# Attention with relative bias and a mixture of adapters: the last pair's values by key group, the last batch's mixture written out apart, and two batches' mixture moved sooner

## The chip, the cores and the metric

The kernel runs on one core of one Trainium2 chip. The time is device microseconds of that core for one execution. It is the median of several runs; lower is better.

## The reference

Two layers follow one another. First comes attention over 8 batches, 8 heads, 576 positions and 64 dimensions a head, with a bias that depends on the distance of two positions:

```python
scores = scale * np.matmul(q, k.transpose(0, 1, 3, 2))
...
scores = scores + bias.transpose(2, 0, 1)[None, :, :, :]
scores = scores - np.max(scores, axis=-1, keepdims=True)
attn = np.exp(scores)
attn = attn / (np.sum(attn, axis=-1, keepdims=True) + 1e-09)
return np.matmul(attn, v).astype(np.float32)
```

Its output, 4608 rows of 512 columns (8 heads of 64), goes row by row through a mixture of 8 adapters of rank 16, of which the two with the largest logits count:

```python
logits = x @ w_gate
topk = np.argpartition(-logits, K, axis=1)[:, :K]
...
        z = x[mask] @ A[e]
        delta[mask] += w[mask, k, None] * (z @ B[e])
return (x + delta).astype(np.float32)
```

Here w is the softmax over a row's two chosen logits, and K is 2.

## The kernel before

**Tiling.** The work goes by pairs: a pair is one batch and two heads (e = 0 and 1, heads hp and hp + 4), so there are 32 pairs, four to a batch. The 576 positions are 512 and a tail of 64. A pair's scores come in five key groups: groups 0 to 3 are 128 keys each against 512 queries of both heads; group 4 takes the tail's keys and queries together. For each group `qk` makes the scores on TensorE, `expo` (L351) takes the exponential on ScalarE, and `band` (L357) multiplies the biased diagonal band on VectorE. `pv` (L372) multiplies the probabilities by the values, one slot of 128 queries (sl) after the other, over all five key groups; a column of ones beside the values gives the sums. `recip` and `norm` (L408, L416) divide and write x, the attention's output in bf16. It has two accumulators for a pair: part 0 for slots 0 to 2 and part 1 for slot 3 and the tail.

**The mixture of a batch b** follows once its four pairs are done. x must be transposed: by a transposing DMA for batches 1 to 5 (`m_xdma`, L441), by 16 TensorE transposes and two VectorE copies for batches 0, 6 and 7 (`m_x`, L447). The tails of two batches are handled together, with the odd batch (`m_xtail`, L458, in float32 by plain matmuls). Then come `m_logits` (L469: 16 or 20 matmuls, the two largest logits on VectorE), `m_gate` (L490: an exponential on ScalarE, a product on GpSimd, a sum and reciprocal on VectorE, the normalised gate on GpSimd), `m_z` (L510: x times A, weighed by the gate on VectorE), `m_zT` (transposes of z), `m_out` (L537: z times B on TensorE, x added on VectorE, and a transfer of half the rows after every second of four) and `m_outt` (L549) for the tails.

**Order.** It is written by hand. One loop (L605) runs over slots n = 5 i + g, for pair i and group g. A slot issues qk of slot n + 1, the exponential of slot n, then band work of slot n - 1, then the previous pair's `pv`, at g = 1, 2 and 3. The mixture's steps are put into slots by a table of events (`mixture`, L569): at (di, g) after the pair 4 (b + 1). The number d, 3 for batches up to 5 and 2 after that, says how many pairs later the logits stand. What falls behind the last slot runs in order after the loop, which goes five slots past the last exponential.

Each engine takes its instructions in this order and waits where one isn't ready. Score tiles have two buffers in PSUM (L66). All other matmul outputs share four ("acc", L67): transposes, values, logits, z and outputs each take the next of these in turn, and wait until VectorE has read what stood there. Instructions on VectorE go through a recorder, so the profile gives all of them line 87; they are told apart by their tiles: kqT, p (the band), rc, x, xT, m, zt, zT, o, ot.

Of the kernel before, what the change touches and what calls it, by code (L numbers as in the profile page):

```python
# [10 lines left out]
FP32 = mybir.dt.float32  # L11
BF16 = mybir.dt.bfloat16
AX = mybir.AxisListType
ALU = mybir.AluOpType
# [13 lines left out]
def kernel(  # L28
# [14 lines left out]
    nc = tc.nc  # L43
    B, H, S, D = q.shape
    NB = bias_table.shape[0]
    Dm = H * D
    E = moe_w_gate.shape[1]
    r = moe_A.shape[2]
    ER = E * r
    HP = H // 2  # L50
    D1 = D + 1
    scale = 1.0 / float(np.sqrt(D))
    S4 = 512
# [37 lines left out]
    dve = Recorder(nc.vector)  # L91
# [280 lines left out]
    def pv(i, sl):  # L372
# [25 lines left out]
        for g in range(4):  # L398
# [4 lines left out]
        mm(acc[:, c:c + 2, :], p4[:, sl * 128:(sl + 1) * 128],  # L403
           vt[:, hp, :].rearrange("p (e d) -> p e d", e=2), False, True)

    rcs = {}

    def recip(i, part):  # L408
        if i % HP == 0 and part == 0:
            xs[i // HP] = xp.tile([128, 9, HP, D], BF16, name="x", tag="x", bufs=4)  # L410
        n = 6 - 3 * part
        rc = sp.tile([128, n], FP32, name="rc", tag=f"rc{part}")
        dve.reciprocal(rc, pvs[(i, part)][:, :, D])
        rcs[(i, part)] = rc

    def norm(i, part):  # L416
        b, hp = divmod(i, HP)
        n = 6 - 3 * part
        dve.tensor_tensor(xs[b][:, 6 * part:6 * part + n, hp, :],
                          pvs.pop((i, part))[:, :, :D],  # L420
                          rcs.pop((i, part)).unsqueeze(2)
                          .to_broadcast((128, n, D)), op=ALU.mult)

    def x_rows(b):
        return xs[b][:, 0:8].rearrange("p (t e) c d -> p t (e c d)", e=2)

    def x_tail(b):
        return xs[b][:, 8].rearrange("p c d -> p (c d)")
# [9 lines left out]
    def new_xT(b):  # L438
        st[(b, "xT")] = xp.tile([128, 20, 128], BF16, name="xT", tag="xT")
# [16 lines left out]
        dve.tensor_copy(st[(b, "xT")][:, half * 8:half * 8 + 8, :], ps)  # L456

    def m_xtail(b):  # L458
        ps = acp.tile([128, 4, 128], FP32, name="xtps", tag="acc")
        for c in range(4):  # L460
            e, hh = divmod(c, 2)
            for bb in range(2):
                nc.tensor.matmul(ps[:, c, bb * 64:(bb + 1) * 64],
                                 lhsT=x_tail(b - 1 + bb)[:, hh * 128:(hh + 1) * 128],
                                 rhs=ident[:, e * 64:(e + 1) * 64],
                                 start=(c + bb == 0), stop=True, skip_group_check=True)
        dve.tensor_copy(st[(b, "xT")][:, 16:20], ps)

    def m_logits(b):  # L469
        nt, xT = tiles(b), st[(b, "xT")]  # L470
        lp = acp.tile([128, nt, E], FP32, name="lp", tag="acc")
        first = True
        for t in range(nt):
            for c in range(4):
                nc.tensor.matmul(lp[:, t, :], lhsT=xT[:, 4 * t + c, :],
                                 rhs=Wb[:, c, :], start=first, stop=(c == 3),
                                 skip_group_check=True)
                first = False
        m8 = sp.tile([128, nt, 8], FP32, name="m8", tag=f"m8{nt}")
        for t in range(nt):  # L480
            dve.max(out=m8[:, t, :], in_=lp[:, t, :])
        df = sp.tile([128, nt, E], FP32, name="df", tag=f"df{nt}")
        dve.tensor_tensor(df, lp, m8[:, :, 0:1].to_broadcast((128, nt, E)),
                          op=ALU.subtract)
        mk = sp.tile([128, nt, E], FP32, name="mk", tag=f"mk{nt}")
        dve.tensor_tensor(mk, lp, m8[:, :, 1:2].to_broadcast((128, nt, E)),
                          op=ALU.is_ge)
        st[(b, "g")] = dict(df=df, mk=mk)

    def m_gate(b, part):  # L490
        nt, d = tiles(b), st[(b, "g")]
        if part == 0:
            ex = sp.tile([128, nt, E], FP32, name="ex", tag=f"ex{nt}")
            nc.scalar.activation(ex, d["df"], ACT.Exp)
            d["ex"] = ex
        elif part == 1:
            nc.gpsimd.tensor_tensor(d["mk"], d["mk"], d["ex"], op=ALU.mult)
        elif part == 2:
            sm = sp.tile([128, nt], FP32, name="sm", tag=f"sm{nt}")
            dve.tensor_reduce(sm, d["mk"], axis=AX.X, op=ALU.add)  # L500
            dve.reciprocal(sm, sm)
            d["sm"] = sm
        else:
            gate = sp.tile([128, nt, E], BF16, name="gate", tag=f"gate{nt}")
            nc.gpsimd.tensor_tensor(
                gate, d["mk"], d["sm"].unsqueeze(2).to_broadcast((128, nt, E)),
                op=ALU.mult)
            d["gate"] = gate
# [55 lines left out]
            nc.sync.dma_start(out=out[n0:n0 + 64, :], in_=o[e * 64:(e + 1) * 64])  # L564


    events = {}

    def mixture(b):  # L569
        tail = b % 2 == 1  # L570
        i0 = HP * (b + 1)

        def at_slot(di, g, f, *a):
            events.setdefault(5 * (i0 + di) + g, []).append((f, a))

        if 0 < b < B - 2:
            at_slot(0, 4, m_xdma, b)
        else:
            at_slot(0, 4, m_x, b, 0)
            at_slot(0, 4, m_x, b, 1)  # L580
        if tail:
            at_slot(1, 4, m_xtail, b)
        d = 3 if b < B - 2 else 2
        at_slot(d, 0, m_logits, b)
        for n in range(4):
            at_slot(d, (2, 3, 4, 4)[n], m_gate, b, n)
        at_slot(d + 1, 0, m_z, b, 0, 4)
        if tail:
            at_slot(d + 1, 2, m_z, b, 4, 5)
        at_slot(d + 1, 4, m_zT, b)  # L590
        at_slot(d + 2, 0, m_out, b, 0)
        at_slot(d + 2, 2, m_out, b, 1)
        at_slot(d + 3, 0, m_out, b, 2)
        at_slot(d + 3, 2, m_out, b, 3)
        if tail:
            at_slot(d + 4, 4, m_outt, b)
# [5 lines left out]
        mixture(b)  # L602
    transposes(0)
    qk(0)
    for n in range(NG + 5):  # L605
        i, g = divmod(n, 5)
        b, hp = divmod(i, HP)
        nb = b + 1
        if n + 1 < NG:
            qk(n + 1)  # L610
        if n < NG:
            expo(n)

        if i >= HP and nb < B and hp in (1, 2) and g in (0, 2):
            behind_dve(load_v(nb, (2 * hp - 2 + g // 2,))[0])
        if b + 2 < B and (hp, g) in ((2, 4), (3, 1)):
            if g == 4:
                alloc_kq(b + 2)
            behind_dve(load_kq(b + 2, ws=(int(g == 1),))[0])
        if hp == 3 and g < 4 and nb + 1 < B:  # L620
            load_tail(nb + 1, g // 2, g % 2)
        if hp == 1 and g in (1, 3) and nb < B:
            load_tail(nb, 2, g // 2)
        if 22 <= n < 27:
            load_weights(n - 22)
        if n in (11, 13, 15, 18):
            cast_v((11, 13, 15, 18).index(n), dve)
        if n in (8, 10, 12, 15):
            band_table((8, 10, 12, 15).index(n))
        if 9 <= n < 15:  # L630
            band(2 * n - 18)
            band(2 * n - 17)
        if 16 <= n <= NG:
            band(n - 1)
        if n == 10 or g == 1 and hp == 0 and 0 < i < NPAIR:
            tail_scores(b)
        if n in (12, 13):
            load_tail(1, n - 12, 0)
            load_tail(1, n - 12, 1)
        if n == 6:  # L640
            tail_transposes(0)
        if n in (0, 3):
            cast_kq(1 + n // 3, 0, dve)
            cast_kq(1 + n // 3, 1, dve)
        if g == 0 and 3 <= i + 2 < NPAIR:
            behind_dve(cast_kq(i + 2, 0))
        if (n in (0, 4, 12) or g == 0 and i > 2) and i + 1 < NPAIR:
            transposes({0: 1, 4: 2, 12: 3}.get(n, i + 1))
        if n == 18 or g == 2 and hp == 2 and 0 < b < B - 1:
            tail_transposes(nb)  # L650
        if 13 <= n < 19:
            for sl in ((3, 4), (0, 1, 2))[n % 2]:
                pv((n - 13) // 2, sl)
            recip((n - 13) // 2, 1 - n % 2)
            norm((n - 13) // 2, 1 - n % 2)
        if i > 3:
            if g == 1:
                pv(i - 1, 0)
                pv(i - 1, 1)
            if g == 2:  # L660
                pv(i - 1, 2)
                recip(i - 1, 0)
            if g == 3:
                pv(i - 1, 3)
                pv(i - 1, 4)
                recip(i - 1, 1)
        if g == 2 and 3 <= i + 2 < NPAIR:
            behind_dve(cast_kq(i + 2, 1))
        if g == 2 and HP <= i < NPAIR:
            behind_dve(cast_v(i))  # L670
        if i > 3 and g in (2, 4):
            norm(i - 1, g // 2 - 1)
        for f, a in events.pop(n, ()):
            f(*a)
# [33 lines left out]
```

The softmax here doesn't subtract the row's maximum and nothing guards it: scores larger than these inputs give would overflow.

## Time and profile before

| | before |
|---|---|
| time, median of 3 runs | 210.39 us (209.14 to 211.6) |
| span of the profiled run | 209.4 us, mean TensorE clock 0.952 |
| TensorE matmul busy | 178.6 us (85%) |
| VectorE busy | 172.5 us (82%) |
| ScalarE busy | 160.7 us (77%), of it 152.9 in 160 exponentials |
| GpSimd busy | 103.3 us (49%) |
| DMA | 40.65 MB, 194 GB/s on average |

The span runs from the first to the last instruction. Busy is the time in which an engine executes; for TensorE it can flatter, since matmuls overlap. A share is over the whole span, whose stages have different limits: a start of some 40 us in which the loads come in, a loop, and an end after the last exponential. A line of a timeline or of the chain gives start and length in us, the engine, the source line, the operation, and then output and input by the program's names. A bracket at its end gives how long the engine stood idle before it and which instruction released it.

### The profile page before, as it was taken

The page shows a single profiled execution, that of the slowest core. Times are in us where ns is not written, and L with a number is a line of the kernel's source. Part 1 is how long each engine was busy: PE and PEld are TensorE (multiplying, and loading weights), DVE is VectorE, ACT ScalarE, POOL GpSimd, SP SyncE. Part 2 cuts the span into 40 slices and gives each one's busy share as a digit, 9 for nine tenths or more (in the row PEclk, how much of TensorE's full clock was granted, in tenths as well). Part 3 has the DMA queues.
Part 4 walks back from the last instruction along what each step waited for, and adds up shares of the span by engine and source line. Part 5 has one row for each costly group of instructions (what it writes and reads, how often), then busy time and mean ns, then how long its engine had stood idle before and what let it go on. Part 6 is the DMA issues. An engine that isn't in the chain of part 4 may idle for free.

```text
span 209.4 us, 6933 instructions
## 1 busy us (share of the span) xinstructions
PE 178.6 (85%) x2768; PEld 120.5 (58%) x2768; DVE 172.5 (82%) x450; ACT 160.7 (77%) x187; POOL 103.3 (49%) x187
## 2 busy tenths in 40 slices
PE   1784399898889999999999999999997999998560
PEld 0241287666666666666666666667665676666420
DVE  3524699999878997999889998999798679988862
ACT  4698356989989898999799889987997688991000
POOL 7693494796745375447554664466543341120000
PEclk9999679999999999999999999999999699999955
DMA  5989999799889699999999999999999640222406
GB/s 186 220 167 160 297 293 157 202 276 151 103 274 235 115 216 261 292 179 214 264 310 164 176 220 304 196 175 203 281 263 167 189 139 3 103 103 53 200 0 250
DMA packets 84504, 40.65 MB, mean 194 GB/s; under 512 B 64240, under 2 KB 81808, under 8 KB 84472
## 3 DMA queue, kind: packets, MB, share of 16 engines
q1 hardware_dynamic: 66080, 38.02, 73.8%
q0 software_dynamic: 18112, 2.17, 19.9%
q8 instruction: 21, 0.34, 0.7%
q14 instruction: 11, 0.09, 0.2%
q10 hardware_dynamic: 280, 0.02, 0.1%
HBM read 29.97 MB, written 9.45 MB: 188 GB/s over the span
## 4 chain that ended last, share of the span: by engine, by line
PE 37%; DVE 22%; DMA 18%; ACT 12%; issue 4%; POOL 3%; SPq 2%; DVEq 0%; POOLq 0%; ACTq 0%
ACT p L354 10%; PE pv L382 9%; PE sc L333 9%; DVE p L87 6%; DMA xT<-x 6%; DVE o L87 4%; DMA kf<-in_k_dram 4%; PE kqps L293 4%; PE sc L339 4%; DMA Wb<-in_moe_w_gate_dram 4%; PE zp L519 3%; DVE x L87 3%; DMA vf<-in_v_dram 3%; DVE kqT L87 2%; DMA g_d<-gg 2%
## 5 line engine op out<-in xcount | busy, mean ns | idle before, releaser
L354 ACT ACTIVATE p<-sc 128x1024 bf16<-128x1024 f32 x160 | 152.9, 1028 | 18.9 <-PE sc L339 9.6
L87 DVE TENSOR_TENSOR p<-p,M 128x512 bf16<-128x512 bf16 (+1 forms) x128 | 66.3, 540 | 0.1
L382 PE MATMUL pv<-vn,p 128*128 128x65 bf16 (+1 forms) x1280 | 60.0, 197 | 0.0
L382 PEld LDWEIGHTS <-p 128*128 128x128 bf16 (+1 forms) x1408 | 51.2, 101 | 14.4 <-issue 9.5
L333 PE MATMUL sc<-kqT 64*128 64x512 bf16 x256 | 51.7, 403 | 7.9 <-ACT p L354 7.1
L146 POOL CAST kqn<-qf 128x512 bf16<-128x512 f32 x29 | 18.1, 624 | 43.6 <-DVE rc L87 41.8
L87 DVE TENSOR_TENSOR x<-pv,rc 128x384 bf16<-128x384 f32 x64 | 29.0, 453 | 1.2
L146 POOL CAST kqn<-kf 128x512 bf16<-128x512 f32 x29 | 18.4, 634 | 23.5 <-DVE xT L87 6.3
L293 PE MATMUL kqps<-ident,kqn 128*128 128x128 bf16 x256 | 21.9, 231 | 8.2 <-DVE kqn L87 4.7
L87 DVE COPY kqT<-kqps 128x1024 bf16<-128x1024 bf16 x32 | 21.9, 684 | 8.4 <-PE kqps L293 8.1
L382 PE MATMUL pv<-vt,p 128*128 128x130 bf16 x128 | 28.5, 222 | 0.0
L333 PEld LDWEIGHTS <-kqT 64*128 64x128 bf16 x256 | 12.7, 94 | 24.8 <-issue 17.9
L293 PEld LDWEIGHTS <-kqn 128*128 128x128 bf16 x256 | 15.5, 102 | 16.7 <-DVE kqn L87 5.9
L150 POOL CAST vn<-vf 128x512 bf16<-128x512 f32 x28 | 21.2, 758 | 6.2 <-DVE rc L87 6.2
L87 DVE TENSOR_TENSOR o<-dl,x 128x512 f32<-128x512 f32 x32 | 21.5, 681 | 1.2 <-PE dl L540 1.2
L87 DVE RECIPROCAL rc<-pv 128x6 f32<-128x6 f32 x64 | 11.6, 181 | 7.0 <-PE pv L382 6.8
L339 PEld LDWEIGHTS <-kqT 128*128 128x128 bf16 x128 | 10.1, 99 | 7.6 <-issue 2.7
L540 PE MATMUL dl<-Bb,zT 128*128 128x512 bf16 x32 | 12.4, 411 | 1.5 <-DVE zT L87 1.5
L339 PE MATMUL sc<-kqT,tlT 128*128 128x512 bf16 x32 | 12.4, 389 | 1.1 <-ACT p L354 1.0
L339 PE MATMUL sc<-tlT,kqT 128*128 128x128 bf16 x128 | 12.6, 222 | 0.0
L339 PE MATMUL sc<-B,ident 128*128 128x128 bf16 x64 | 9.1, 222 | 1.8 <-POOL B L258 1.8
L136 POOL DMA_DIRECT2D vt<-in_v_dram x16 | 10.1, 636 | 0.0
(78 smaller groups left out, 180.2 us busy)
## 6 DMA issues: line engine op xcount, KB each, us to landing
vf<-in_v_dram SPq DMA_DIRECT2D x128, 64.0 KB, 4.0
out_dram<-o SPq DMA_DIRECT2D x16, 512.0 KB, 3.0
kf<-in_k_dram SPq DMA_DIRECT2D x6, 1024.0 KB, 7.1
qf<-in_q_dram SPq DMA_DIRECT2D x6, 1024.0 KB, 10.1
kf<-in_k_dram SPq DMA_DIRECT2D x8, 256.0 KB, 4.5
qf<-in_q_dram SPq DMA_DIRECT2D x8, 256.0 KB, 4.8
out_dram<-ot SPq DMA_DIRECT2D x8, 128.0 KB, 5.0
Mr<-g_d SPq DMA_DIRECT2D x4, 192.0 KB, 4.5
```

Source lines behind the costliest of these rows:

```text
L87: self.last = f(*a, **kw)
L136: nc.gpsimd.dma_start(out=o, in_=sr[e])
L146: return (eng or nc.gpsimd).tensor_copy(o, s)
L150: return (eng or nc.gpsimd).tensor_copy(vns[b % 2][:, :, hp:H:HP, :D], vfs[b][:, :, hp:H:HP, :])
L293: nc.tensor.transpose(o, n[:, w, j], ident)
L333: nc.tensor.matmul(sc[:, h * 512:(h + 1) * 512], lhsT=t[s, 0, g * 128:(g + 1) * 128], rhs=t[s, 1, :], start=True, stop=True)
L339: nc.tensor.matmul(o, lhsT=lhsT, rhs=rhs, start=start, stop=stop, skip_group_check=True)
L354: nc.scalar.activation(p, scs.pop(n), ACT.Exp, scale=scale)
L382: nc.tensor.matmul(o, lhsT=lhsT, rhs=rhs, start=start, stop=stop, skip_group_check=True)
L519: nc.tensor.matmul(zp[:, t - t0, :], lhsT=xT[:, 4 * t + c, :], rhs=Ab[:, c, :], start=(t == t0 and c == 0), stop=(c == 3), skip_group_chec ...
L540: nc.tensor.matmul(ps, lhsT=zT[:, t, :], rhs=Bb, start=True, stop=True)
```

## The change

There are three parts.

1. The last pair (31): its values are multiplied by key group as the probabilities come (`pv_group`), two groups in each of the last two slots of the loop and only group 4 behind the last exponential. Both parts are then normalised in a row.
2. The last batch (7) has its mixture written out apart (`m_last`). The column blocks that come from its first two pairs (even blocks) are transposed already at pair 31, the others (odd blocks) at the end (`m_xh`), with the copy shared between VectorE and ScalarE. z is multiplied before the gate is known. The first two tiles are weighed with the gate not yet divided by its sum, which is made good when x is added; the other tiles take the divided gate, and their x is added by TensorE and the result copied by ScalarE. Each quarter of the rows leaves by a transfer of its own, from the scores' buffers.
3. Batches 5 and 6: batch 5 is transposed on TensorE instead of by DMA, and for both the logits stand at (1, 3) instead of (3, 0) and (2, 0), with the later steps following sooner. Their outputs end within the loop. All tails (odd batches) are now transposed in bf16 by 4 TensorE transposes instead of 8 float32 matmuls.

The loop now ends one slot past the last exponential. The diff, cut:

```diff
+    def pv_group(i, g):
...
+        for sl in range(4):
+            acc, c = pvs[(i, sl // 3)], 2 * (sl % 3)
+            if g == 4:
+                mm(acc[:, c:c + 2, :], p4[:, sl * 128:(sl + 1) * 128],
+                   vt[:, hp, :].rearrange("p (e d) -> p e d", e=2), False)
+                continue
+            for e in range(2):
+                o = e * 512 + sl * 128
+                mm(acc[:, c + e, :], probs[(i, g)][:, o:o + 128],
+                   vn[:, g, e * HP + hp, :], sl % 3 == 0 and g == 0 and e == 0)
...
     def m_xtail(b):
-        ps = acp.tile([128, 4, 128], FP32, name="xtps", tag="acc")
...
+        ps = acp.tile([128, 2, 2, 128], BF16, name="xtps", tag="acc")
+        for hh in range(2):
             for bb in range(2):
...
+                nc.tensor.transpose(ps[:, hh, bb, :],
+                                    x_tail(b - 1 + bb)[:, hh * 128:(hh + 1) * 128], ident)
...
+    def m_xh(b, odd):
...
+        for t in range(4):
+            for h in range(2):
+                c = 2 * h + odd
+                nc.tensor.transpose(ps[:, t, h, :], x[:, t, c * 128:(c + 1) * 128], ident)
...
+        if odd:
+            dve.tensor_copy(o[:, 0:2], ps[:, 0:2])
+            nc.scalar.copy(o[:, 2:4], ps[:, 2:4])
+        else:
+            dve.tensor_copy(o, ps)
...
+    def m_last(b):
+        m_xh(b, 1)
+        m_xtail(b)
+        m_logits(b)
...
+        zps = [acp.tile([128, n, ER], FP32, name="zp", tag="acc") for n in (4, 1)]
...
+        m_gate(b, 0)
+        wt = d["mk"]
+        dve.tensor_tensor(wt, wt, d["ex"], op=ALU.mult)
...
+        weigh(0, 2, zps[0][:, 0:2], wt[:, 0:2])
...
+        dve.tensor_reduce(sm, wt, axis=AX.X, op=ALU.add)
+        dve.reciprocal(sm, sm)
...
+        weigh(2, 4, zps[0][:, 2:4], wn[:, 0:2])
+        weigh(4, 5, zps[1], wn[:, 2:3])
...
+        for t0, t1 in ((0, 2), (2, 5)):
+            ps = acp.tile([128, t1 - t0, 128], BF16, name="ztps", tag="acc")
+            for t in range(t0, t1):
+                nc.tensor.transpose(ps[:, t - t0, :], zt[:, t, :], ident)
+            (nc.scalar.copy if t0 else dve.tensor_copy)(zT[:, t0:t1], ps)
+            dl = scp.tile([128, 2, Dm], FP32, name="sc", tag="sc")
+            for t in range(t0, t0 + 2):
+                nc.tensor.matmul(dl[:, t - t0], lhsT=zT[:, t, :], rhs=Bb, start=True,
+                                 stop=(t0 == 0))
+                if t0:
+                    nc.tensor.matmul(dl[:, t - t0], lhsT=ident, rhs=x[:, t], start=False,
+                                     stop=True)
+            for t in range(t0, t0 + 2):
+                if t0:
+                    nc.scalar.copy(o[:, t], dl[:, t - t0])
+                else:
+                    dve.scalar_tensor_tensor(o[:, t], dl[:, t], sm[:, t:t + 1], x[:, t],
+                                             op0=ALU.mult, op1=ALU.add)
+                nc.sync.dma_start(out=orr[:, t], in_=o[:, t])
+        st[(b, "zT")] = zT
+        m_outt(b)
...
-        if 0 < b < B - 2:
+        if b == B - 1:
+            at_slot(-1, 0, m_xh, b, 0)
+            at_slot(0, 1, m_last, b)
+            return
+        if 0 < b < B - 3:
             at_slot(0, 4, m_xdma, b)
...
+        if b >= B - 3:
+            if tail:
+                at_slot(1, 1, m_xtail, b)
+            at_slot(1, 3, m_logits, b)
+            for n in range(4):
+                at_slot(*((1, 4), (2, 0), (2, 0), (2, 0))[n], m_gate, b, n)
+            at_slot(2, 1, m_z, b, 0, 4)
+            if tail:
+                at_slot(2, 2, m_z, b, 4, 5)
+            at_slot(2, 4, m_zT, b)
+            for t in range(4):
+                at_slot(3, (0, 1, 3, 4)[t], m_out, b, t)
+            if tail:
+                at_slot(4, 1, m_outt, b)
+            return
...
-    for n in range(NG + 5):
+    for n in range(NG + 1):
...
+        if n >= NG - 2:
+            for pg in ((0, 1), (2, 3), (4,))[n - NG + 2]:
+                pv_group(NPAIR - 1, pg)
+        if n == NG:
+            for part in range(2):
+                recip(i - 1, part)
+                norm(i - 1, part)
```

## The prediction

> **What bounds the kernel now.** I read the page's picture in 40 slices first, to divide the run into a loop and an end.
>
> ```profile
> PE   1784399898889999999999999999997999998560
> ...
> DVE  3524699999878997999889998999798679988862
> ACT  4698356989989898999799889987997688991000
> ...
> PEclk9999679999999999999999999999999699999955
> ```
>
> A slice is 5.2 us. From about 40 us on, TensorE, VectorE and ScalarE are all nine tenths busy; ScalarE then has nothing for the last 20 us. Two things stand out: a dip of the TensorE clock in slice 32, far inside the loop, and the half clock of the last two slices. So I asked for busy times by stage (columns: length, then busy time and count of PE, weight loads, DVE, ACT, POOL, then clock, DMA share, GB/s).
>
> ```profile
> 122.20:143.60 21.40, 20.82 (x339) 14.22 (x337) 19.49 (x53) 19.68 (x23) 11.54 (x21) 1.00 1.24 224
> ...
> 161.00:167.40 6.40, 5.13 (x79) 3.53 (x80) 3.93 (x15) 4.01 (x6) 2.06 (x3) 0.73 0.68 173
> 167.40:189.50 22.10, 21.46 (x353) 15.11 (x352) 20.01 (x57) 20.04 (x22) 5.93 (x13) 1.00 0.23 83
> 189.50:209.40 19.90, 10.01 (x136) 6.24 (x132) 12.36 (x32) 0.24 (x2) 0.52 (x2) 0.76 0.37 133
> ```
>
> The first row is one ordinary batch (four pairs): TensorE 20.82 of 21.40 us, VectorE 19.49, ScalarE 19.68. TensorE sets the pace, with the other two some 10% behind: 0.6 us a batch is all the room TensorE has. The last row is the end: 19.9 us in which no engine is full, so a chain sets it. The 161 to 167.4 row is the clock dip. The chain of waits says what is in it (start, length, what), and ScalarE's timeline what it cost.
>
> ```profile
> 150.27 11.72 DMA xT<-x
> 161.98 0.05 issue
> 162.03 0.68 PE lp L475 x20
> ```
>
> ```profile
> 158.94 2.85 ACT L354 ACTIVATE p<-sc 128x1024 bf16<-128x1024 f32 x3 [0.62 <-PE sc L339]
> 163.29 1.02 ACT L354 ACTIVATE p<-sc 128x1024 bf16<-128x1024 f32 x1 [1.49 <-PE sc L333]
> ...
> 165.10 1.02 ACT L354 ACTIVATE p<-sc 128x1024 bf16<-128x1024 f32 x1 [0.67 <-PE sc L333]
> 166.36 2.86 ACT L354 ACTIVATE p<-sc 128x1024 bf16<-128x1024 f32 x3 [0.23 <-PE sc L339]
> ...
> 182.69 6.81 ACT L354 ACTIVATE p<-sc 128x1024 bf16<-128x1024 f32 x7 [0.16 <-ACT ex L494]
> ```
>
> Batch 5's transposing DMA lands 11.7 us after its issue begins, behind the moment at which its logits stand first in TensorE's queue. TensorE waits 1.07 us, its clock falls (0.73 on average until 167.4), and ScalarE loses 1.49 + 0.67 + 0.23 = 2.4 us. In batches 1 to 4 the logits start at 75.1, 96.5, 118.0 and 139.3 with no such wait. The last exponential ends at 182.69 + 6.81 = 189.5 us; call this T. From there the chain of waits goes on:
>
> ```profile
> 192.38 0.56 DVE x L87
> ...
> 195.21 1.20 DVE o L87 x2
> 196.41 0.61 DVE xT L87
> 197.02 0.05 issue
> 197.06 0.27 PE lp L475 x4
> ...
> 204.11 0.68 DVE o L87
> 204.79 0.60 DVEq L703
> ```
>
> Between T and the last logits (T + 7.8) stand not only the last pair's values and transposes but batch 6's outputs ("o", 0.68 us each). The tail's copy ends at 205.4 (T + 15.9), and 4.0 us of output transfer follow.
>
> **What the Trainium skill says.** "TensorE: Matmul & The Clock Gate", section "HAM oscillation", warns of TensorE gaps over about 3.4 us; here a wait of 1.07 us was enough to be followed by the slow clock, so the trace is stricter. The same page, section "Part 4: PE-mode transpose", gives about 275 ns for a transpose inside a kernel; the trace has 16 of them in 0.89 us (56 ns each, pipelined), which I use. "ScalarE: Activation LUTs", section "What ACT_TABLE_LOAD costs", gives 186 ns + 0.833 ns per element: 612 ns for 512, and the trace has 597 for the 128x512 activation from PSUM; I use it for the new ScalarE copies (an estimate of 506 ns for 384). "VectorE: DVE Perf Modes", section "The perf-mode tier table", caps a float PSUM source lower than a bf16 one: the trace agrees, 678 against 414 ns for 512 elements.
>
> **The change, part by part.**
>
> *Batch 5 without the DMA.* Takes away the wait and the slow clock: -2.4 us at T. Its two transposes add 16 matmuls, 0.89 us, and two VectorE copies, 2 x 0.68 = 1.36 us.
>
> *Batch 5's and 6's mixture sooner.* Inside the loop moving costs nothing in the sum; what counts is what crosses T. Batch 6's transposes of z (0.32 us on TensorE, 0.41 on VectorE), four output matmuls (0.22 to 0.32 each, 1.0 together) and three of its four output additions (2.04 on VectorE) come to stand before T, and batch 5's tail copy (0.68, at 189.75 in the trace) with them.
>
> *Last batch's even column blocks at pair 31.* 8 transposes, 0.45 us, and one copy, 0.68, before T instead of after.
>
> *Last pair's values by key group.* Before, its 46 matmuls stand behind T although four fifths of their inputs are ready. 32 of them (9 take 0.30 us, so 1.1) go before T. The rest, some 0.5 us, stay behind the last exponential.
>
> *Tail transposes in bf16.* 4 instead of 8 matmuls, -0.1 us before T; its copy 0.41 instead of 0.68.
>
> Sum for TensorE before T: 0.89 + 0.32 + 1.0 + 0.45 + 1.1 - 0.1 = 3.6 us. With the engine 97% full I give no credit for its idle time (0.6 us a batch, two batches: at best 1.2). T moves by -2.4 + 3.6 = +1.2, to 190.7. Check for VectorE: 39.7 us busy from 143.6 to 189.5, plus 1.36 + 0.41 + 2.04 + 0.68 + 0.68 - 0.27 = 4.9, gives 44.6 in 47.1 us, 95%: possible, but nearly a second bound. If it holds TensorE up through the four accumulators, T is 192; with all TensorE room used it is 189.8.
>
> *Added waits.* All of batch 5's and 6's gate runs in one slot: VectorE's sum now waits for GpSimd's product, with the bias products queued behind it; but GpSimd's cast ahead (0.61) and product (0.26) are shorter than VectorE's own copy and its wait, so about nothing. In the last slot batch 6's fourth output matmul waits for an accumulator that VectorE's normalisation of pair 30 frees; key group 4 and so everything later is behind it. I put that matmul at T, and its addition on VectorE (0.68) ahead of the last reciprocal.
>
> *From T to the last logits.* The fourth addition ends at T + 1.0; reciprocal and normalisations (0.19 + 0.56 + 0.17 + 0.35, the trace's own) to T + 2.3; transposes to T + 2.65; half the odd copy on VectorE (0.41) and the tail's (0.41), the other half on ScalarE (0.6) beside them, to T + 3.2; the last logits (0.27) T + 3.5. Before: T + 7.8. Gain 4.3.
>
> *From the logits to the tail's copy.* Before 8.1 us (197.3 to 205.4). After, in a row: maxima 0.5, difference 0.2, exponential with its handover 0.35, product now on VectorE 0.25, first z weighing 0.4, sum, reciprocal and gate 0.65, two weighings 0.6, first copy of z 0.3: 3.3. TensorE then does two output matmuls and only behind them the other three transposes: at the half clock (0.43 a matmul, as 201.67 to 203.56 shows) 1.35; ScalarE copies z, 0.55; then four matmuls, the tail's one and its four (1.7 + 1.1), and the tail's copy 0.7. About 8.6: a loss of 0.5, since the outputs' additions, now shared with ScalarE, no longer bound it but TensorE's row does. At full clock it would be 7.3.
>
> *The transfer.* Before, 1.3 MB goes out in the last 5 us; after, the pieces leave as they come and the last 256 KB meet an emptier queue. Bounded by 4.0 (as now) and 3.0 (the landing time of the larger outputs inside the loop, on the page's list of transfers); I take 3.2: -0.8.
>
> Sum: +1.2 - 4.3 + 0.5 - 0.8 = -3.4 us; 210.39 - 3.4 = 207.0.
>
> **Rivals.**
>
> *More room than I grant.* TensorE's idle shares absorb 1.2 us of the added work and the end runs at full clock: -3.4 - 1.2 - 1.3 gives 204.5. For it: ScalarE runs unbroken in the last seven slots, so TensorE keeps up there. Against: its busy share is 97% in every stage.
>
> *VectorE takes the place of TensorE.* T at 192.4 instead of 190.7, and its queue runs late into the end, 0.7 more: 209.4, no change. For it: 95% by my own sum, and a stretch (172.4 to 177.4) in which it is already 5.00 of 5.00 us busy just where batch 6's transposes sit, as batch 5's now will. Against: most of its work has a slot or more of slack.
>
> *A new stall in the loop (slower).* Pair 24 gets 0.89 us more on top of z, tail scores and transposes, pair 26 gets batch 5's z with the next tail transposes: if a wait on an accumulator idles TensorE for a microsecond and the clock falls as it did at 162, twice, that is 2 x 2.4 lost, and the end may gain only 3.2: +1.2 + 4.8 - 3.2 = +2.8, 213.2. Against: pair 28 of the kernel before has the same load with no clock dip.
>
> **How the numbers follow.** My forecast 0.55, more room 0.22, VectorE 0.14, new stall 0.09. Range: the loop from +0.3 to +2.5, the end from -6.0 to -3.2, and 0.7 for the spread of the times before (209.14 to 211.6); taken together not all at their worst, 204.2 to 209.4. Faster by over 1% means under 208.3: most of my forecast and all of the second, 0.77; within 1% the rest of it and VectorE's case, 0.14; slower 0.09.
>
> **What would show it.** The TensorE clock at 1.0 through 160 to 168, no wait for a transposing DMA by batch 5's logits; last exponential at about 190.7 (189.8 to 192); no output addition of batch 6 after T + 1.0; last logits at T + 3.5; the second group of output matmuls at half clock; last copy at T + 12.1. I am wrong if ScalarE shows new idle time of over a microsecond in pairs 24 to 27, if VectorE's queue reaches T more than a microsecond late, or if other runs of the kernel before have no stall in batch 5, so that nothing is removed.

## The result, and the profile after

The changed kernel takes 217.58 us (median, 214.95 to 217.97) against 210.07 for the kernel before: ratio 1.032, with a 95% interval of 1.022 to 1.043. Measured a second time, beside the experiments (e5), the ratio was 1.028 (1.019 to 1.036). All ratios leave out the executions that are over 1.5% above the fastest of their kernel, on both sides, so a ratio can differ from the quotient of two medians. The forecast was 207.0, faster. It is slower.

The picture in 40 slices of the changed kernel (a slice is 5.4 us), with the rows of TensorE, ScalarE and the clock:

```profile
PE   1586398898999999999999899989989899886860
...
ACT  3499356899989898989798889876877898783110
...
PEclk9998579999999999999999999979999999999558
```

The half clock of the end is still there (slices 38 and 39), the dip inside the loop has moved from slice 32 to slice 27, and after it no engine keeps its row of nines: from slice 27 to 36 TensorE shows 8 or 9 and ScalarE mostly 6 to 8.

To compare kernels I cut each trace at three marks that every kernel has: ScalarE's tail exponential of pair 24, that of pair 28, and the end T of the last exponential. A is pairs 24 to 27, B is pair 28 to T, C is T to the end. First A and B of the kernel before (its C is the last row of stages in the prediction), then A of the kernel of experiment e4, which has no late DMA, then the changed kernel (busy times by stage; columns as in the prediction):

```profile
146.41:170.18 23.77, 21.90 (x347) 14.91 (x344) 19.44 (x54) 19.66 (x23) 9.55 (x16) 0.93 0.98 222
170.18:189.50 19.32, 18.72 (x319) 13.03 (x315) 17.61 (x51) 18.22 (x20) 4.66 (x9) 1.00 0.17 68
```

```profile
145.68:166.93 21.25, 20.45 (x347) 14.15 (x344) 19.33 (x54) 19.52 (x23) 9.55 (x16) 1.00 0.98 221
```

```profile
150.38:175.01 24.63, 22.86 (x370) 15.88 (x369) 22.44 (x61) 20.20 (x22) 9.18 (x16) 1.00 0.72 208
175.01:196.13 21.12, 18.80 (x331) 13.49 (x329) 17.65 (x49) 18.13 (x20) 5.65 (x10) 1.00 0.17 56
196.13:215.70 19.57, 10.25 (x108) 6.27 (x106) 8.79 (x29) 2.38 (x5) 0.00 (x0) 0.70 0.30 104
```

A of the kernel before holds the stall; without one it is 21.25 us (e4). So A is 3.4 us longer, B 1.8 longer, and C, where the forecast had 4.6 to gain, 0.3 shorter. In A and B TensorE is idle for 1.8 and 2.3 us, with its clock at 1.00, against 0.8 in A of e4 and 0.6 in B of the kernel before. (In e5's trace of the same kernel, which has a few more matmul records, the idle times are 1.4 and 2.1.) In A there is also more work, 22.9 us busy against 20.45. B's busy time on TensorE has hardly grown (18.72 to 18.80, 19.02 in e5): what grew there is waiting.

The forecast -2.4 us for the stall did not come either. The chain of waits of the changed kernel, 20 us earlier than in the one before:

```profile
130.29 11.48 DMA xT<-x
141.77 0.05 issue
141.81 0.56 PE lp L525 x16
```

Batch 4's transposing DMA is late now (and batch 3's by a little), before anything of the change runs but the tail transposes of batches 1 and 3. So the changed kernel's trace holds a stall of the same kind as the one before; A, B and C, 4.9 us in sum over the undisturbed ones (those without a late DMA), are what is the change's own. The two traces are 6.3 us apart (209.4 and 215.7): these 4.9, 3.2 for late DMAs and 0.8 for a later start of the loop in the changed kernel's, less 2.5 for the late DMA in the one before. The traced execution of the kernel before lies 1.1 us above its median, which gives the 7.5 us between the medians.

### The profile page after: what moved, and what is told of

The parts are those of the page before. It is cut to its first block, busy times and chain, and to the rows that moved or that the text cites. A ratio compares the mean times of both kernels' runs of the same rounds, so it can differ in the third digit from the quotient of the medians.

```text
span 215.7 us, 6931 instructions
## 1 busy us (share of the span) xinstructions
PE 181.2 (84%) x2755; PEld 123.3 (57%) x2770; DVE 170.9 (79%) x453; ACT 163.5 (76%) x191; POOL 103.3 (48%) x185
## 4 chain that ended last, share of the span: by engine, by line
PE 42%; DMA 22%; ACT 14%; DVE 8%; issue 7%; POOL 3%; SPq 2%; POOLq 0%; another core or an unknown queue 0%; ACTq 0%; DVEq 0%
ACT p L354 12%; DMA xT<-x 11%; PE pv L382 10%; PE sc L333 10%; PE sc L339 5%; PE kqps L293 4%; PE zp L569 3%; DMA vf<-in_v_dram 3%; DMA qf<-in_q_dram 3%; DMA tl<-in_q_dram 3%; DMA kf<-in_k_dram 2%; DVE o L87 2%; DVE p L87 1%; DVE x L87 1%; PE tps L302 1%
## 5 line engine op out<-in xcount | busy, mean ns | idle before, releaser
L87 DVE TENSOR_TENSOR p<-p,M 128x512 bf16<-128x512 bf16 (+1 forms) x128 | 65.2, 528 | 0.1
L333 PE MATMUL sc<-kqT 64*128 64x512 bf16 x256 | 51.1, 401 | 11.0 <-ACT p L354 9.8
L382 PE MATMUL pv<-vn,p 128*128 128x65 bf16 x1240 | 58.2, 197 | 0.3
L382 PEld LDWEIGHTS <-p 128*128 128x128 bf16 x1364 | 49.5, 101 | 14.0 <-issue 10.0
L382 PE MATMUL pv<-vt,p 128*128 128x130 bf16 x124 | 27.5, 222 | 0.0
L150 POOL CAST vn<-vf 128x512 bf16<-128x512 f32 x28 | 21.9, 783 | 8.0 <-DVE rc L87 7.6
L87 DVE TENSOR_TENSOR o<-dl,x 128x512 f32<-128x512 f32 x28 | 19.1, 682 | 1.7 <-PE dl L590 0.7
L339 PE MATMUL sc<-tlT,kqT 128*128 128x128 bf16 x128 | 13.3, 231 | 0.0
L136 POOL DMA_DIRECT2D tl<-in_k_dram x16 | 10.0, 628 | 0.1
L136 POOL DMA_DIRECT2D tl<-in_q_dram x16 | 9.9, 617 | 0.0
```

The lines of the kernel that those rows point to most:

```text
L87: self.last = f(*a, **kw)
L136: nc.gpsimd.dma_start(out=o, in_=sr[e])
L150: return (eng or nc.gpsimd).tensor_copy(vns[b % 2][:, :, hp:H:HP, :D], vfs[b][:, :, hp:H:HP, :])
L333: nc.tensor.matmul(sc[:, h * 512:(h + 1) * 512], lhsT=t[s, 0, g * 128:(g + 1) * 128], rhs=t[s, 1, :], start=True, stop=True)
L339: nc.tensor.matmul(o, lhsT=lhsT, rhs=rhs, start=start, stop=stop, skip_group_check=True)
L382: nc.tensor.matmul(o, lhsT=lhsT, rhs=rhs, start=start, stop=stop, skip_group_check=True)
```

## The experiments

| kernel | A | B | C | ratio to before (95%) |
|---|---|---|---|---|
| before | 23.77 (21.25 with no late DMA) | 19.32 | 19.90 | |
| changed | 24.63 | 21.12 | 19.57 | 1.032 (1.022 to 1.043) |
| e1 batch 5 on TensorE | 22.15 | 19.33 | 20.02 | 1.003 (0.999 to 1.006) |
| e2 part 3 alone | 24.63 | 20.67 | 17.54 | 1.005 (1.001 to 1.009) |
| e3 changed, spaced | 23.63 | 20.45 | 19.34 | 1.007 (1.003 to 1.011) |
| e4 parts 1 and 2 alone | 21.25 | 19.77 | 20.60 | none (see below) |
| e5 changed again | 24.62 | 21.12 | 19.68 | 1.028 (1.019 to 1.036) |
| e6 changed, values late | 24.63 | 21.12 | 18.26 | 1.022 (1.011 to 1.033) |
| e7 changed, outputs on ScalarE | 24.63 | 21.12 | 17.49 | 1.016 (1.009 to 1.022) |
| e12 changed, batch 5 left alone | 21.25 | 21.67 | 19.93 | 1.016 (1.009 to 1.023) |
| e9 before, late logits | 21.66 | 19.64 | 20.21 | 0.999 (0.995 to 1.003) |
| e8 best | 21.66 | 20.07 | 16.88 | 0.982 (0.973 to 0.992) |
| e10 best, values late | 22.91 (one late DMA) | 20.07 | 16.26 | 0.981 (0.970 to 0.991) |
| e11 best with part 3 | 25.35 | 20.46 | 15.48 | 0.997 (0.993 to 1.000) |

A, B and C (us) are from one profiled execution each; e5 shows how well they repeat (24.62, 21.12, 19.68 against 24.63, 21.12, 19.57).

**e1, batch 5 on TensorE.**

```diff
-        if 0 < b < B - 2:
+        if 0 < b < B - 3:
```

> The kernel before with one edit: batch 5 transposed on TensorE, at its old slots. Theory A (late transposing DMAs are not tied to batch 5: in the trace of the changed kernel batch 4's is late, 11.5 us, and costs ScalarE 2.2 us): the time stays within 1 us of 210.1, the trace shows no stall in batch 5 and, at some other batch, may show one. Theory B (the stall belongs to batch 5, as the prediction had it): 2.4 us less for the stall, 0.9 more for the transposes, 208.6.

Theory A held: no gain. A has 22.15 us, 0.9 over the undisturbed 21.25: what 16 transposes were priced at. The stall is not batch 5's own. Over all traces, TensorE waits for a transposing DMA at batch 4 in e1, e2, e5, e6 and e11 (0.2 to 1.0 us), at 3 and 4 in the changed kernel and e7, at 4 and 5 in e10, and at 5 alone in the kernel before; in e3, e4, e8, e9 and e12 at none, though all of these but e3 have batch 5's DMA. The DMA of batches 3 to 5 lands about when its logits come up, and which one misses changes from trace to trace.

**e2, part 3 alone.** The kernel before with the changed kernel's events for batches 5 and 6 and its tail transposes.

> The kernel before with part 3 alone: batches 5 and 6 sooner, batch 5 on TensorE, tails by 4 transposes; last pair and last batch as before. Theory A (the loop pays for 2.2 us of TensorE work that crosses the last exponential, plus 1.5 to 2.5 us because each step of a mixture now stands right behind the step that it needs, so that ScalarE and VectorE wait at the head of their queues): last exponential 3.7 to 4.7 us later than 189.5, waits of ScalarE for VectorE's difference df of 0.7 us and more, end 2 to 3 us shorter, time 211 to 212.5. Theory B (close spacing costs nothing, only added work counts): last exponential 2.2 later at most, time 207 to 209.5.

A is that of the changed kernel to the hundredth, and B is 1.35 us longer than in the kernel before: 4.7 us together over the undisturbed stretches, the upper end of theory A. (T itself, 192.5, is only 3.0 us late, because it is set against a T with a stall of 2.4 in it, and has a wait of 0.9 at batch 4 of its own.) C is 2.4 us shorter, since batch 6's outputs are gone from it. The sum is a loss of 0.5%, at the edge of what can be told: part 3 moves time from C into A and B and pays for the way.

**e3, wider spacing.**

```diff
-                at_slot(*((1, 4), (2, 0), (2, 0), (2, 0))[n], m_gate, b, n)
-            at_slot(2, 1, m_z, b, 0, 4)
+                at_slot(2, (0, 1, 2, 2)[n], m_gate, b, n)
+            at_slot(2, 3, m_z, b, 0, 4)
...
-            at_slot(2, 4, m_zT, b)
+            at_slot(3, 0, m_zT, b)
             for t in range(4):
-                at_slot(3, (0, 1, 3, 4)[t], m_out, b, t)
+                at_slot(3, (1, 2, 3, 4)[t], m_out, b, t)
```

> The changed kernel with the gate's steps of batches 5 and 6 one to two slots further from the logits (exponential of the gate at (2,0), product (2,1), sum and gate (2,2), z (2,3) and (2,4), its transposes (3,0), outputs (3,1) to (3,4)). Theory A (close spacing stops ScalarE and VectorE at the head of their queues): ScalarE's two waits for df (0.85 and 0.69 us) go, VectorE's waits for z (2.5 us in three) shrink, last exponential 1.5 to 2.5 us sooner against the same starting point, time 215 to 216. Theory B (only the added work counts): within 0.5 us of the changed kernel, 217 to 218.

A gives 1.0 us back and B 0.7: 1.67 together, as theory A has it. The ratio fell by more, from 1.028 (e5) to 1.007. The trace of e3 has no late DMA; whether that holds for its other executions, and explains the rest, isn't known. The mechanism is in ScalarE's timeline. Changed kernel:

```profile
157.54 2.19 ACT L354 ACTIVATE p<-sc 128x1024 bf16<-128x1024 f32 x2 [0.23 <-PE sc L333]
160.59 0.24 ACT L544 ACTIVATE ex<-df 128x40 f32<-128x40 f32 x1 [0.85 <-DVE df L87]
160.73 2.83 ACT L354 ACTIVATE p<-sc 128x1024 bf16<-128x1024 f32 x3
...
184.94 0.23 ACT L544 ACTIVATE ex<-df 128x32 f32<-128x32 f32 x1 [0.69 <-DVE mk L87]
```

And TensorE in the same kernel:

```profile
159.72 0.61 PE L333 MATMUL sc<-kqT 64*128 64x512 bf16 x4
...
161.79 0.39 PE L333 MATMUL sc<-kqT 64*128 64x512 bf16 x2 [0.70 <-ACT p L354]
...
186.13 0.39 PE L333 MATMUL sc<-kqT 64*128 64x512 bf16 x2 [0.85 <-ACT p L354]
```

The gate's small exponential (0.24 us) stands one slot behind the logits. It needs VectorE's difference, which needs the logits; ScalarE takes its queue in order, so the next attention exponential stands behind it. ScalarE is idle for 0.85 us, for more than half of it with the scores ready, which TensorE made from 159.72 on. Then the score buffers come free late, and TensorE waits 0.70 us for ScalarE. In e3 the same exponential waits for nothing:

```profile
157.36 0.23 ACT L544 ACTIVATE ex<-df 128x40 f32<-128x40 f32 x1
```

VectorE's waits for z, 2.5 us in three in A and B of the changed kernel, fall to 1.0 in two. A of the changed kernel in its second trace (e5), then A of e3:

```profile
148.18:172.80 24.62, 23.23 (x372) 15.88 (x369) 22.42 (x61) 20.20 (x22) 9.20 (x16) 1.00 0.78 221
```

```profile
146.68:170.31 23.63, 23.17 (x372) 15.92 (x369) 22.15 (x61) 20.25 (x22) 8.65 (x15) 1.00 0.79 221
```

TensorE is as long busy and 1.0 us less idle. From the start of A to the end of the last pair's scores (148.18 to 192.81 and 146.68 to 189.65) it is busy for 41.3 us in both, and idle for 3.3 in e5 and 1.7 in e3. What spacing gives back is waiting, not work.

**e4, parts 1 and 2 alone.** The changed kernel with batches 5 and 6 as in the one before; batch 6's four outputs stand between the last normalisation and the last mixture.

> The changed kernel without part 3: batches 5 and 6 as in the kernel before (batch 5 by DMA, tails by 8 matmuls), but batch 6's four outputs, which fall behind the last exponential, all stand between the last normalisation and the last batch's mixture. Parts 1 and 2 stay. Theory A (the time was lost in part 3; the end's own rewrite gains, even with these four outputs of 0.68 us in it): last exponential 1 to 1.5 us later than in the kernel before, the end 1.5 to 3 us shorter, time 208 to 210. Theory C (the end's rewrite itself loses: values by key group and the even blocks in the last slots hold up TensorE): last exponential 2.5 us later or more, time 211 to 213.

Four executions spread too far for a ratio (209.0 to 214.1, median 210.7, beside 211.1). The trace decides: B is 0.45 us longer than in the kernel before, which is the price of the even blocks and no more, so the 32 early matmuls do not hold up the loop: not theory C. But C is 20.6, not shorter: theory A's gain of the end isn't there either. Its four output additions take 2.48 us of VectorE in a row ahead of the last transposes' copies. On top of part 3 the same two parts cost more: from e2 to the changed kernel B grows from 20.67 to 21.12 us and C from 17.54 to 19.57, 2.5 together against 1.15 here. e6 and e7 look for the reason.

**e5, the changed kernel again.**

> The changed kernel itself, on one chip beside the next three, since the times of the kernel before spread from 208.7 to 215.5 us in the first experiments. Theory A (about 4.9 us of the 7.5 are its own: pairs 24 to 27 cost 24.6 instead of 21.3 us, the last stretch to the last exponential 21.1 instead of 19.3, the end 19.6 instead of 19.9; the rest was late transposing DMAs of batches 3 and 4 and a late start in that execution): the same three stretches within 0.2 us, and 2 to 3 us above the kernel before. Theory B (all 7.5 us are its own): 6 us or more above it.

The three stretches repeat to 0.1 us, as theory A has it, but the ratio is theory B's: 2.8% of some 210 us is 5.9, with an interval of 4 to 7.6. The medians of all executions, 214.92 and 211.26, are 3.7 us apart, between the two theories. A, B and C together are 4.9 us over the undisturbed ones, within the ratio's interval. Theory A had the stretches right and their sum wrong: it took the stall off for the changed kernel alone, and this trace, too, has a late DMA, at batch 4 (1.0 us of wait).

**e6, the last pair's values late.**

```diff
-        if n >= NG - 2:
-            for pg in ((0, 1), (2, 3), (4,))[n - NG + 2]:
-                pv_group(NPAIR - 1, pg)
+        if n == NG:
+            for sl in range(5):
+                pv(i - 1, sl)
```

> The changed kernel with the last pair's values behind the last exponential again (all 46 matmuls), everything else kept. Theory A (the 32 early matmuls cost the last slots about their 1.1 us and the wait for GpSimd's cast, and give 1.1 back behind the last exponential): last exponential 0.8 to 1.5 us sooner, end longer by as much, time within 0.7 us of the changed kernel. Theory C (in the last slots they stand in front of batch 6's output matmuls, whose additions hold up VectorE's band work and the normalisation, so that they lose more than they give): 1 us or more faster than the changed kernel.

Theory C's sign: B is unchanged at 21.12, so the 32 matmuls cost nothing ahead of T, and C is 1.4 us shorter without them. Part 1 loses in this place. The times overlap (213.9 against 214.9), so the stretch carries this, not the ratio. Why is seen with the next one.

**e7, batch 6's last two outputs behind group 4, on ScalarE.**

```diff
+        nc.tensor.matmul(ps, lhsT=zT[:, t, :], rhs=Bb, start=True, stop=False)
+        nc.tensor.matmul(ps, lhsT=ident, rhs=x_rows(b)[:, t], start=False, stop=True)
...
+        nc.scalar.copy(o[:, t], ps)
```

> The changed kernel with batch 6's last two outputs moved behind key group 4: TensorE adds x, ScalarE, which has nothing to do there, copies. Theory A (in the changed kernel these two outputs stand ahead of the last reciprocal on VectorE and wait in turn for TensorE, so that it starts 2.9 us after the last exponential instead of 1.0): last reciprocal sooner than T + 1.5, last logits at T + 4.5 instead of T + 6.1, time 1 to 2 us less. Theory B (the end is set by TensorE at the half clock, whatever VectorE does): within 0.5 us.

C is 2.1 us shorter, and the ratio falls from 1.028 to 1.016. Theory A: most of the gain is there before the last logits. VectorE around T, first in the changed kernel (T = 196.13), then in e7 (T = 195.61):

```profile
196.67 0.69 DVE L87 TENSOR_TENSOR o<-dl,x 128x512 f32<-128x512 f32 x1 [0.47 <-PE dl L590]
197.28 0.42 DVE L87 TENSOR_TENSOR p<-p,M 128x512 bf16<-128x512 bf16 x1
...
198.43 0.69 DVE L87 TENSOR_TENSOR o<-dl,x 128x512 f32<-128x512 f32 x1 [0.47 <-remote]
199.04 0.19 DVE L87 RECIPROCAL rc<-pv 128x6 f32<-128x6 f32 x1
```

```profile
195.62 0.39 DVE L87 TENSOR_TENSOR p<-p,M 128x512 bf16<-128x512 bf16 x1
...
196.69 0.20 DVE L87 RECIPROCAL rc<-pv 128x6 f32<-128x6 f32 x1 [0.42 <-PE pv L416]
```

And TensorE in the changed kernel, from the end of the last scores on:

```profile
194.73 0.28 PE L339 MATMUL sc<-B,ident 128*128 128x128 bf16 x2
...
195.76 0.65 PE L416 MATMUL pv<-vn,p 128*128 128x65 bf16 x16 [0.19 <-POOL vn L150]
196.26 0.38 PE L590 MATMUL dl<-Bb,zT 128*128 128x512 bf16 x1
...
197.75 0.42 PE L416 MATMUL pv<-vn,p 128*128 128x65 bf16 x8 [0.87 <-DVE p L87]
```

In the changed kernel the last band product (p) stands behind the third output addition (o), which waits for its matmul (dl); that matmul stands on TensorE behind the values of groups 0 and 1. The values of group 3 need the band product, the fourth output matmul stands behind them, and its addition ahead of the last reciprocal. Two in-order queues wait for each other in turn: the reciprocal starts at T + 2.9. Without the two outputs it starts at T + 1.1, and the last logits come at T + 4.4 instead of T + 6.1. e6 cuts the same knot at its other end, by taking the early values out of TensorE's queue: there the reciprocal starts at T + 2.0 and the last logits come at T + 5.2.

**e12, batch 5 left alone.** The changed kernel, with batch 5 by DMA and at its old slots.

```diff
-        if 0 < b < B - 3:
+        if 0 < b < B - 2:
...
-        if b >= B - 3:
+        if b >= B - 2:
```

> The changed kernel with batch 5 left as in the kernel before (by DMA, at its old slots); only batch 6 is sooner, with the spacing of the changed kernel. Theory A (what batch 5 has moved into pairs 24 to 27 is paid there in full, and leaving it in place costs the last stretch less than that): pairs 24 to 27 at 21.3 us where no DMA is late (23.8 where one is), against 24.6; the last stretch 22 to 23 against 21.1; the two together 1 to 2.5 us less than in the changed kernel. Theory B (moving batch 5's steps between stretches is a zero sum apart from its transposes, 0.9): together 0.9 less, with the last stretch at 23.5 or more.

A returns to 21.25 us, B rises only to 21.67. Together 42.9 instead of 45.7: batch 5's part costs 2.8 us, more than either theory gave it. Up to the end of the last scores TensorE has 39.3 us of work here and 41.3 in e5, so 2.0 of the 2.8 is work: 0.9 its transposes (e1), and 0.7 the five matmuls of batch 5's tail outputs, which here and in the kernel before stand behind the last scores and in the changed kernel ahead of them; the rest was not traced. The other 0.8 is idle time (2.5 against 3.3).

**e9, the kernel before with later logits.**

```diff
+        late = 2 if 0 < b < B - 2 else 0
...
-        at_slot(d, 0, m_logits, b)
+        at_late(d, 0, m_logits, b)
```

> The kernel before with the logits of batches 1 to 5, and every later step of theirs, two slots later, so that a transposing DMA may land some 2 us later before TensorE waits for it. Theory A (which batch's DMA is late differs from execution to execution; each late one costs about 2.4 us with the slow clock that follows): no wait for it in the trace, lowest time as before (208.7), median lower by 1 to 2 us and the spread smaller. Theory B (late DMAs are rare and the spread comes from elsewhere): median and spread as before.

Theory A came out in what it named: the trace has no wait for a transposing DMA, the median is 1.9 us lower (209.35 against 211.26), the lowest time nearly the same (207.75 and 208.07), and one of 12 executions lies above 211 us, against 8 of 15 of the kernel before. The ratio, 0.999, leaves these high ones out and says only that the others gain nothing. That late DMAs make the high ones is likely, not shown. The traces of e7 and e10 happen to be of the highest execution of their kernels (214.87 and 208.63 us), and each holds two waits for such DMAs, of 0.96 and 1.00 us and of 0.83 and 1.07. e10 has these later logits too, so two slots do not rule a late DMA out.

**e8, e10 and e11, a version drawn from these.** e8 keeps e9's loop, with the tails transposed by 8 matmuls as in the kernel before, and parts 1 and 2; the outputs of batch 6 are made as in e7, three of them behind group 4 and the last behind the tail's transposes; in the last mixture the second group of z is turned before the outputs wait, x is added by VectorE, and ScalarE copies z and the tail.

```diff
+        turn(0, 2)
+        delta(0)
+        turn(2, 5)
+        delta(1)
+        delta(2)
+        delta(3)
```

> A version drawn from the experiments: loop as in the kernel before with logits of batches 1 to 5 two slots later; parts 1 and 2 kept; batch 6 at its old slots, its four outputs behind key group 4 with x added by TensorE and the copy on ScalarE; the last batch's z turned before its outputs wait for it, x added by VectorE, copies of z and of the tail on ScalarE. Theory A: last exponential near 186.3 (0.5 after the kernel with late logits alone, for the even blocks), end 16.5 us instead of 19.9, time 203.5 to 206. Theory C (early values hold up the last slots whatever stands beside them): end above 18, time above 207.

Ratio 0.982: 1.8% faster than the kernel before (median 206.5 beside 212.2), the first version whose ratio lies clear below 1. Theory A's stretches came out (T at 186.0, C 16.9), and the median lies half a microsecond above its range. Its B and C:

```profile
165.95:186.02 20.07, 19.80 (x348) 14.56 (x345) 18.38 (x52) 18.00 (x20) 5.48 (x10) 1.00 0.25 91
186.02:202.90 16.88, 9.05 (x130) 5.59 (x126) 8.99 (x30) 4.31 (x9) 0.00 (x0) 0.92 0.46 156
```

B holds more TensorE work than the changed kernel's (19.80 against 18.80, 19.02 in e5) in 1.05 us less. The clock of C is 0.92 instead of 0.70, and the last outputs are spaced 0.22 us and not 0.43. Batch 6's eight matmuls fill time in which TensorE stood idle in the changed kernel; that they keep up the clock was not tested apart from the other edits, and e10 has a shorter C at 0.80.

> The same version with the last pair's values behind the last exponential, all 46 matmuls. Theory A (early values cost only where batch 6's output matmuls stand among them; now they don't): 1 us slower than with early values, from an end longer by 1 us. Theory C: 1 us faster, as between the changed kernel and its version with late values (18.3 against 19.6 us of end).

Neither: 0.981 can't be told from e8's 0.982. C is 0.6 us shorter in the trace, so even with batch 6's outputs out of the way the early values show no gain.

> The same version again but with part 3 in it: batch 5 by TensorE, batches 5 and 6 sooner at the wider spacing, batch 6's first two outputs in the last slots and its other two on ScalarE at the end; logits of batches 1 to 4 late. Theory A (part 3 costs the loop 2.4 us in pairs 24 to 27 and 0.7 to 1.1 after it, and can give back only what batch 6's outputs cost at the end): 2 to 3 us slower than the version without it. Theory B (part 3 was only badly spaced): within 0.5 us of it or faster.

Theory A: 0.997 against 0.982, some 3 us. A is 3.7 us longer and B 0.4, C 1.4 shorter. In A nearly all of it is work: TensorE is busy for 24.87 us against 21.03. Part 3 loses even when spaced and repaired.

## Why the prediction was wrong, point by point

Three steps failed, in order of size: the end, where 4.6 us were to be gained and 0.3 were; the stall, whose 2.4 us were not batch 5's to take away; and the waits in the loop, which were put at about nothing and took 1.9.

**"Takes away the wait and the slow clock: -2.4 us at T."** Wrong. I took a wait seen in one trace for a property of batch 5. e1 and the waits at batches 3 and 4 show that it is not. Nor does each late DMA cost so much. Against the same stretch with no late DMA, the loop loses 2.4 to 2.5 us where the clock falls after the wait (kernel before, changed kernel, e7's second) and 1.0 to 1.4 after waits of 0.82 to 1.07 us where it doesn't (e2, e5, e6, e7's first, e10). So "a wait of 1.07 us was enough" for the slow clock does not hold: e10 has one of 1.07 with the clock at 1.00 behind it. What makes a given DMA late was not settled.

**"Sum for TensorE before T", 3.6 us.** The size of the added work was nearly right, with other terms than I had listed. Up to the end of the last scores, with no late DMA, TensorE is busy for 38.06 us (A of e4, B of e1) and in the changed kernel for 41.33 (e5): 3.3 more. The transposes cost 0.9 as said (e1) and the even blocks 0.45 as said (e4). The early values cost nothing instead of 1.1 (e6), since they stand behind the last scores in TensorE's queue (195.76 against 195.01) and can't delay T; so does batch 6's third output matmul (196.26). What I left out are the five matmuls of batch 5's tail outputs, 0.7, which came from behind the last scores to ahead of them. Batch 6's steps cost 0.8 of work (e12's 39.3 less e4's 38.5) and another 1.1 of waiting.

**"Moving costs nothing in the sum" and "Added waits ... about nothing".** This is the step that failed in the loop: it counted TensorE's work, and the waits not at all. The undisturbed A and B grew by 5.2, and up to the end of the last scores TensorE is idle for 3.3 us instead of 1.4. I looked at VectorE's wait for GpSimd and missed two others of the same kind: ScalarE's gate exponential in front of the attention's, and VectorE's weighing of z in front of the band work. Wider spacing gives 1.67 us back (e3), nearly all of the 1.9.

**"From T to the last logits", T + 3.5.** Measured T + 6.1. "The fourth addition ends at T + 1.0" failed: it ended at T + 3.0, behind the knot of output matmuls, band product and early values. Without the last two outputs the logits come at T + 4.4 (e7); the 0.9 us that then remain were not traced. I had seen the fourth matmul's wait for an accumulator and gave it no time.

**"From the logits to the tail's copy", 8.6.** 9.2 (202.2 to 211.4), mechanism as told, but for one wait: the products of z take 2.29 us here (1.28 in e7, at full clock), and their first weighing waits 0.46 us for them. The second turning of z, behind the first outputs:

```profile
206.70 0.53 PE L657 MATMUL ztps<-ident,zt 128*128 128x128 bf16 x3
...
207.80 0.61 PE L661 MATMUL sc<-Bb,zT 128*128 128x512 bf16 x1 [0.57 <-ACT zT L658]
```

**"The transfer", 3.2.** 4.3 from the tail's copy to the end; it was 4.0 before. Smaller and earlier pieces gave nothing here. With the 2.6 of the logits and the 0.6 of the tail's copy these 1.1 us make up the 4.3 that the end fell short.

**The rivals.** The slower one (0.09) had the sign and the place, pairs 24 to 27, but not the cause: the clock stayed at 1.00 in A and B, and ScalarE's queue, not an accumulator, began the waits there. (One wait for an accumulator stands in B, 0.66 us at 191.87, until VectorE has copied batch 6's turned z.) VectorE did not become the bound: 22.4 of 24.6 us busy in A, 17.7 of 21.1 in B. Two of the signs of error that I had named came: new idle time of ScalarE in pairs 24 to 27, and traces with batch 5's DMA and no stall at it (e4 and e12; with later logits e8 and e9).

## What to carry to other kernels

A step moved to just behind the one that it needs makes its engine wait at the head of an in-order queue, and everything behind waits with it: leave a slot or two, and check every engine's queue, above all that of the engine which paces the loop. Work queued behind the last scores can't delay them: when adding up what a change puts ahead of a point, go by the place in the queue and not by the step's name. Where an output or a copy that nobody waits for stands ahead of the last chain, move it behind, onto an engine that is idle there (e7, e8). One trace's stall is one draw: look for it in a second trace before counting on its removal.

## What the runs showed of the hardware that was not expected

The length of a wait does not tell whether TensorE's clock falls after it. It fell after waits for a transposing DMA of 1.07 us (kernel before: 0.73 on average from 161 to 167.4), 0.80 (changed kernel: 0.64 from 141.8 to 146.5) and 1.00 (e7: 0.63 from 141.4 to 146). It stayed at 1.00 after waits of 1.07 and 0.83 (e10), 0.97 (e5), 0.96 (e7's first), 0.89 (e2), 0.82 (e6) and 0.59 (changed kernel), all of them ahead of a batch's logits, and after one of 0.85 for ScalarE at 186.13 in the changed kernel. What decides was not found.

Where TensorE waited for it, a DMA transpose of 128 x 2048 elements landed 10.9 to 13.7 us after its issue began. Over all traces its issue alone held the queue for 1.4 to 9.6 us.

From the last copy to the end of the span passed 4.0 to 4.6 us (kernel before, changed kernel, e4, e8, e10), though the kernel before moved 250 GB/s in the last of its 40 slices and the changed kernel 146.
